# DeltaNet and soft-MoE on one Trainium2 core: another order for VectorE's queue, an own tile for half of the inverse, another start

## The chip, the cores and the metric

The kernel runs on one core of one Trainium2 chip. A time is device microseconds of one execution; a kernel's time is the median of its runs. A profiled run is one such execution with a trace, and its span is about 1.7 us shorter than its time. Runs count as slow when they are over 1.5% above the fastest of the same kernel; slow runs stay out of ratios, but medians take in all runs. PE is TensorE, DVE is VectorE, ACT is ScalarE, POOL is GpSimd, SP is SyncE; SPq is SyncE's DMA queue.

## The reference, cut to what matters

```python
# q, k, v: (B=4, H=8, S=768, D=48) float32, beta: (4, 8, 768)
k_n = k / (norm(k, axis=-1) + 1e-6)
for t in range(S):                          # one state of 48x48 per (b, h)
    y[:, :, t] = q[:, :, t] . state
    v_old = state . k_n[:, :, t]
    state = state + beta[t] * outer(k_n[t], v[t] - v_old)
x = y, transposed to (3072, 384)
# soft mixture of experts: 8 experts, 4 slots each, hidden size 1024
logits = x @ phi                            # (3072, 32)
d = softmax(logits, axis=0); slot_input = d.T @ x
slot_out[e] = relu(slot_input[e] @ w1[e]) @ w2[e]
out = softmax(logits, axis=1) @ slot_out
```

## The kernel before

The sequence is cut into 24 chunks of 32 tokens. Within a chunk the recurrence becomes a triangular system of 32x32, and its inverse is built on VectorE for four chunks (a group) at a time, one group ahead. A chunk itself is a chain over four engines:

```python
rest()      # PE: psR = K . S (state), then DVE: R = V - psR
read()      # PE: psY = Q . S
solve()     # PE: psR = inverse . R ; ACT: U = psR
update()    # PE: psS += K^T . U    ; ACT: S = psS   (the next chunk's state)
outputs()   # PE: psY += A . U      ; ACT: Y = psY
```

R is VectorE's only step in that chain. VectorE's other work is the inverse: 95 instructions for each group, products `prE`, `prM`, `prL` and the additions of them, then two back transposes; the preparation of the next inverse (a spreading transpose `lb`, the norms of k, which need a square root from ScalarE); and steps of the routing.

```python
# the second half of the inverse: a product, then its addition, 16 times
def la(j):
    tt = full(st["tt"])
    pr["l", j] = outer("prL", [HC - j, HC], tt[:, HC + j:C, HC + j].unsqueeze(2),
                       st["nm"][:, j, :].unsqueeze(1))      # outer: tile tag, bufs=2
def ls(j):
    add(full(st["tt"])[:, HC + j:C, 0:HC], pr["l", j], ALU.add)

# which share of the inverse's steps stands in which of a chunk's three places
share = [(0.0, 0.10, 0.11), (0.11, 0.10, 0.10), (0.09, 0.08, 0.08), (0.11, 0.12, 0.0)]

# one chunk of the main loop, in the order in which each engine's queue is filled
hook("head")                    # routing
drain(EL[c][0])                 # inverse, place 0; for c == 0 the norms come first
rest(); read()
...
hook("act"); drain(EL[c][1])    # routing, then inverse, place 1
if follow and x > GC:
    follow[0]["spread"]()
solve()
...
hook("mid"); hook("vec")
drain(EL[c][2])                 # inverse, place 2
update(); outputs()
...
# query blocks that chunk x asks for
queries = {0: (), 1: (9, 10, 11), 2: (12, 13), 3: (14,), 4: (15, 16)}
```

At the start the first loads go to SyncE and ScalarE, beta comes in 16 small loads on GpSimd, and V0 to V3 are loaded by SyncE. At the end the experts' weights `w1t` and `w2t` (15 loads of 1.5 MB) take memory that the loop's buffers leave.

Of the kernel before, what the change touches and what calls it, by code (L numbers as in the profile page):

```python
# [16 lines left out]
def kernel(  # L17
# [83 lines left out]
    load_k(2, nc.scalar)  # L101
    load_k(1)
    load_k(3, nc.scalar)

    one = cpool.tile([P, 1], F32, name="one")
    nc.vector.memset(one, 1.0)
    nc.scalar.preload_act_table_set("natural_log_exp_and_others")
    load_q(0)
    load_k(4)
    load_q(4)  # L110
    load_v(0)
# [18 lines left out]

    bb = cpool.tile([P, NG, C], F32, name="bb")
    for h in range(4):
        for c in range(GC):
            p0 = C * h + U * c
            nc.gpsimd.dma_start(
                out=bb[p0:p0 + U],
                in_=beta.rearrange("b (g h) (n c t) -> h c (b g) n t", h=4, c=GC, t=C)[h, c])
# [10 lines left out]

    psS = psp.tile([P, 4, 512], F32, name="psS")
    psR = psp.tile([P, 512], F32, name="psR")  # L150
    psY = psp.tile([P, 512], F32, name="psY")
    St = [wk.tile([P, 4, B, GD], F32, name=f"S{i}", bufs=1) for i in range(2)]
    for t in St:
        nc.vector.memset(t, 0.0)
# [76 lines left out]
    def invert(n):  # L231
# [17 lines left out]
        def clear():  # L249
            st["nm"] = wk.tile([P, HC, HC], F32, name="nm", tag="nm", bufs=1)  # L250
            nc.gpsimd.memset(st["nm"], 0.0)  # L251
# [54 lines left out]
        def steps():  # L306
# [27 lines left out]
            def la(j):  # L334
                tt = full(st["tt"])
                pr["l", j] = outer("prL", [HC - j, HC], tt[:, HC + j:C, HC + j].unsqueeze(2),
                                   st["nm"][:, j, :].unsqueeze(1))

            def ls(j):
                add(full(st["tt"])[:, HC + j:C, 0:HC], pr["l", j], ALU.add)  # L340
# [11 lines left out]
            for j in range(HC + 1):  # L352
                if j < HC:
                    put(HC * (HC - j), lambda j=j: la(j))
                if j > 0:
                    put(HC * (HC + 1 - j), lambda j=j - 1: ls(j))
            return out
# [117 lines left out]
    def route(n, Yn, yT):  # L475
# [103 lines left out]
        def collect(first):  # L579
# [4 lines left out]
            else:  # L584
# [5 lines left out]
                dict(head=[maxima], mid=[over_rows, by_tokens], vec=[rows_max, over_slots],  # L590
                     end=[spread_max, slots_exp]),
                dict(head=[run_max, shares], act=[rows_exp], end=[repeat, heads]),
# [17 lines left out]
    share = [(0.0, 0.10, 0.11), (0.11, 0.10, 0.10), (0.09, 0.08, 0.08), (0.11, 0.12, 0.0)]  # L610

    def plan(n):
# [3 lines left out]
        if n > 1:  # L616
            at[0][0] += [f["norms"]]
        todo, done, total = f["steps"], 0.0, 0.0
        whole = sum(t[0] for t in todo)
        i = 0  # L620
        for c in range(GC):
            for p in range(PLACES):
                total += share[c][p] * whole
                while i < len(todo) and done + todo[i][0] / 2 < total:
                    done += todo[i][0]
                    at[c][p].append(todo[i][1])
                    i += 1
        at[2][2] += [lambda: f["back"](0)]
        at[3][1] += [t[1] for t in todo[i:]]
        at[3][2] += [lambda: f["back"](1)]  # L630
# [5 lines left out]
    pre = {}  # L636
    f0 = invert(0)
    f0["unit"]()
    for cc in range(4):
        pre[cc] = Prep(cc)  # L640
        pre[cc].alone(0, cc % 2)
        if cc:
            pre[cc - 1].products(0, 1)
    pre[3].products(0, 1)
    f0["spread"]()
    f0["root"]()
# [3 lines left out]
    load_v(1)  # L650
# [16 lines left out]
    load_v(2)  # L667
    load_q(3)
    load_k(9)
    load_v(3)  # L670
# [32 lines left out]
    queries = {0: (), 1: (9, 10, 11), 2: (12, 13), 3: (14,), 4: (15, 16)}  # L703
# [8 lines left out]
    for x in range(NCH):  # L712
# [23 lines left out]
        rest, solve, read, update, outputs = chunk(x, Ys[n % 2])  # L736
        hook("head")
        drain(EL[c][0])
# [5 lines left out]
        if x == 0:  # L744
            f["spread"]()
            f["root"]()
            f["norms"]()
        hook("act")
        drain(EL[c][1])
        if follow and x > GC:  # L750
            follow[0]["spread"]()
# [8 lines left out]
        hook("mid")  # L760
        hook("vec")
        if follow and x < GC:
            follow[0]["spread"]()
        drain(EL[c][2])
# [166 lines left out]
```

## Time and profile before

| | before |
|---|---|
| time, median of 3 runs | 383.27 us (376.66 to 384.48) |
| span of the profiled run | 377.8 us, state fast |
| busy: PE, DVE, ACT, POOL | 77%, 59%, 44%, 41% |
| R of chunk 0 starts at | 47.14 us |
| four chunks each, from 0, 4, 8, 12, 16 | 53.33, 43.76, 42.56, 44.43, 37.62 us |
| chunks 20 to 23, no inverse beside them | 22.03 us for three |
| R of chunk 23 to the end (the tail) | 86.93 us |

The table cuts the span at the starts of R, because each chunk has one, 24 in the span. "R(8)" below is the start of R of chunk 8. One more line of the page is needed later. It is the row of moved GB/s in the 40 equal slices of the span (9.4 us each here); the experts' weights are the high figures from the 32nd slice on:

```profile
GB/s 104 92 83 91 81 85 86 89 90 62 80 51 57 50 70 97 88 109 106 35 19 25 23 27 23 13 13 190 3 4 14 391 427 341 340 424 399 6 201 299
```

### The profile page before, as it was taken

The numbers are of one execution on the slowest core, as the hardware profiler recorded it, in microseconds if no ns is written. First come the engines' busy times: TensorE is split into PE (matmuls) and PEld (weight loads), VectorE is DVE, ScalarE is ACT, GpSimd is POOL, SyncE is SP. The second block draws the span as 40 slices with busy tenths as digits, with TensorE's granted clock in tenths as the row PEclk, the third lists the DMA queues.
The fourth block names the chain that finished last, engine by engine and source line by source line (L and its number), as shares of the span: only waits on it lengthen the run. The fifth ranks groups of instructions, "written<-read, shape, count | busy, mean of one in ns | idle before, by whom it ended". The sixth has DMA issues, their size and how long they took to land.

```text
span 377.8 us, 16079 instructions
## 1 busy us (share of the span) xinstructions
PE 289.3 (77%) x6879; PEld 227.0 (60%) x6879; DVE 223.1 (59%) x798; ACT 164.4 (44%) x340; POOL 154.6 (41%) x338
## 2 busy tenths in 40 slices
PE   1866585789587997779787795789988779867784
PEld 0655474677476886668676794677877673312242
DVE  7289989087757777689847987879321120101043
ACT  1353154366356582668454572446466312001032
POOL 8453478564665059350975039856220000000000
PEclk9996569689799698999989898968999969979895
DMA  6555555553433344554111111005000998899058
GB/s 104 92 83 91 81 85 86 89 90 62 80 51 57 50 70 97 88 109 106 35 19 25 23 27 23 13 13 190 3 4 14 391 427 341 340 424 399 6 201 299
DMA packets 85030, 45.23 MB, mean 120 GB/s; under 512 B 79424, under 2 KB 82656, under 8 KB 83040
## 3 DMA queue, kind: packets, MB, share of 16 engines
q1 hardware_dynamic: 82208, 43.67, 43.1%
q8 instruction: 54, 0.88, 1.0%
q10 hardware_dynamic: 2176, 0.39, 0.7%
q0 software_dynamic: 576, 0.15, 0.3%
q14 instruction: 16, 0.13, 0.1%
HBM read 39.47 MB, written 4.72 MB: 117 GB/s over the span
## 4 chain that ended last, share of the span: by engine, by line
PE 48%; DMA 13%; ACT 12%; DVE 12%; SPq 9%; issue 4%; DVEq 0%; ACTq 0%
PE psR L423 8%; SPq L82 7%; PE psS L436 7%; DMA w2t<-in_moe_w_dram 6%; PE pt L574 5%; PE psY L453 4%; ACT S L443 4%; PE pt L194 4%; DMA Q<-in_q_dram 4%; PE pt L471 4%; PE pso L869 3%; PE pt L223 3%; PE psR L409 2%; DVE R L416 2%; PE ph L845 2%
## 5 line engine op out<-in xcount | busy, mean ns | idle before, releaser
L373 POOL TENSOR_SCALAR V<-V,nT 128x48 f32<-128x48 f32 x192 | 89.0, 487 | 38.5 <-DMA V<-in_v_dram 23.7
L381 POOL TENSOR_SCALAR_AFFINE_SELECT Ab<-GQ 32x256 f32<-32x256 f32 x96 | 46.0, 479 | 28.0 <-PE psY L453 23.7
L423 PE MATMUL psR<-R,Tb 64*64 64x48 f32 x768 | 32.1, 241 | 30.0 <-DVE R L416 18.7
L423 PEld LDWEIGHTS psR<-R,Tb 64*64 64x64 f32 x768 | 29.4, 156 | 33.7 <-issue 21.4
L443 ACT ACTIVATE S<-psS 48x768 f32<-48x768 f32 x46 | 37.0, 805 | 27.2 <-PE psS L436 26.9
L223 PE MATMUL pt<-KQ 48*32 48x64 f32 (+1 forms) x1792 | 26.3, 237 | 10.9 <-ACT KQ L210 7.8
L426 ACT ACTIVATE U<-psR 128x384 f32<-128x384 f32 x24 | 11.8, 491 | 51.2 <-PE psR L423 51.2
L223 PEld LDWEIGHTS pt<-KQ 48*32 48x32 f32 x1792 | 21.2, 119 | 17.1 <-ACT KQ L210 9.3
L299 DVE TENSOR_TENSOR prL<-tt,nm 128x256 f32<-128x256 f32 (+7 forms) x96 | 29.1, 308 | 3.1
L453 PE MATMUL psY<-U,Ab 64*64 64x48 f32 x768 | 30.0, 232 | 0.1
L304 DVE TENSOR_TENSOR nm<-nm,prM 128x16 f32<-128x16 f32 (+7 forms) x96 | 29.8, 310 | 0.0
L299 DVE TENSOR_TENSOR prM<-tt,lb 128x16 f32<-128x16 f32 (+7 forms) x96 | 29.4, 306 | 0.1
L304 DVE TENSOR_TENSOR tt<-tt,prL 128x256 f32<-128x256 f32 (+7 forms) x96 | 29.2, 304 | 0.2
L453 PEld LDWEIGHTS psY<-U,Ab 64*64 64x64 f32 x768 | 27.0, 147 | 2.8 <-issue 1.0
L436 PE MATMUL psS<-U,K 32*112 32x96 f32 x736 | 27.9, 296 | 0.1
L436 PEld LDWEIGHTS psS<-U,K 32*112 32x112 f32 x736 | 23.8, 200 | 4.8 <-issue 1.4
L416 DVE TENSOR_TENSOR R<-V,psR 128x384 f32<-128x384 f32 x24 | 13.0, 543 | 21.2 <-PE psR L409 10.3
L227 ACT ACTIVATE GQ<-pt 128x256 f32<-128x256 f32 (+1 forms) x56 | 16.7, 351 | 20.2 <-PE pt L223 20.1
L194 PE MATMUL pt<-ident,Q 128*128 128x128 f32 x72 | 20.4, 317 | 6.6 <-DMA Q<-in_q_dram 6.6
L386 ACT ACTIVATE Tb<-TT,own 128x256 f32<-128x256 f32 x48 | 21.6, 503 | 7.8 <-DVE TT L364 7.8
L299 DVE TENSOR_TENSOR prE<-tt,lb 128x30 f32<-128x30 f32 (+7 forms) x90 | 24.6, 273 | 0.0
L251 POOL MEMSET nm<- 128x256 f32 x6 | 1.9, 311 | 54.5 <-DVE tt L304 51.2
(132 smaller groups left out, 545.9 us busy)
## 6 DMA issues: line engine op xcount, KB each, us to landing
w2t<-in_moe_w_dram SPq DMA_DIRECT2D x8, 1536.0 KB, 19.4
w1t<-in_moe_w_dram SPq DMA_DIRECT2D x7, 1536.0 KB, 11.0
Q<-in_q_dram SPq DMA_DIRECT2D x96, 48.0 KB, 2.7
V<-in_v_dram SPq DMA_DIRECT2D x96, 48.0 KB, 2.4
out_dram<-ob SPq DMA_DIRECT2D x24, 192.0 KB, 2.4
K<-in_k_dram SPq DMA_DIRECT2D x88, 48.0 KB, 2.6
w1t<-in_moe_w_dram SPq DMA_DIRECT2D x3, 512.0 KB, 4.3
K<-in_k_dram ACTq DMA_DIRECT2D x8, 48.0 KB, 3.3
```

The source lines that it names most:

```text
L82: eng.dma_start(out=dst[C * h:C * h + C, :, 0:D], in_=src.rearrange("b (g h) s d -> h s (b g) d", h=4)[h, cc * C:(cc + 1) * C])
L194: nc.tensor.transpose(dst, self.src[a][:, b * G:(b + 1) * G, :].rearrange("p g d -> p (g d)"), ident)
L223: nc.tensor.matmul(pg[g][rh, b], lhsT=kq[r, b, 0, rh], rhs=kq[r, b, a0:a1, rh], start=True, stop=True, skip_group_check=True)
L299: nc.vector.tensor_tensor(pr, a.broadcast_to([P] + shape), b.broadcast_to([P] + shape), op=ALU.mult)
L304: nc.vector.tensor_tensor(dst, dst, pr, op=op)
L373: nc.gpsimd.tensor_scalar(Vt[cc][:, u], Vt[cc][:, u], nT[n][:, c * U + u:c * U + u + 1], None, op0=ALU.mult)
L381: nc.gpsimd.affine_select(out=Ab[cc % NT][r, :, h % 2, :].rearrange("p (b g) t -> p b g t", g=G), in_=GQ[n][r, c, :, :, 1, :], compare_op= ...
L386: nc.scalar.activation(Tb[cc % 2][:, :, x, :], TT[n][:, c * U:(c + 1) * U, :], ACT.Identity, scale=own[:, x:x + 1])
L423: nc.tensor.matmul(pw[half[y], u], lhsT=T[y][:, u], rhs=st["R"][half[y], u], start=(u == 0), stop=True, skip_group_check=True)
L436: nc.tensor.matmul(psS[0:DP + D, h, b * GD:(b + 1) * GD], lhsT=K[hs[h], b * G:(b + 1) * G].rearrange("p g d -> p (g d)")[:, 0:DP + D], rhs ...
L443: nc.scalar.activation(new[r, :, :, g * D:(g + 1) * D], psS[r, :, 0:B * GD].rearrange("p h (b g e) -> p h b g e", b=B, g=G)[:, :, :, g], A ...
L453: nc.tensor.matmul(qs[half[y], b, g], lhsT=at[y][:, u], rhs=st["U"][half[y], u], start=False, stop=True, skip_group_check=True)
```

## The change

The intent is to let nothing stand in VectorE's queue before R that could stand behind it. Before R there remain a share of the inverse's steps and the little routing that stays in "head"; norms, row maxima and slot shares come behind it. The spread moves to the end of the last place. The second half of the inverse gets a tile of its own, `T21`, so that its additions don't write `tt`. At the start, block K3 and V0 to V3 go to GpSimd's queue, beta comes in one load (`bt`), is laid out by PE with a selection matrix (`sel`), and two products of zeros are given to PE before its first block. Query block 9 is asked for a chunk earlier.

```diff
@@ start
 load_k(0)
 load_k(2, nc.scalar)
+load_k(3, nc.gpsimd)
 load_k(1)
-load_k(3, nc.scalar)
...
+bt = wk.tile([C, S], F32, name="bt", tag="dr", bufs=1)
+nc.sync.dma_start(out=bt, in_=beta.rearrange("b h s -> (b h) s"))
-load_v(0)
...
+sel = wk.tile([C, GC, 4, GC, U], F32, name="sel", tag="dT", bufs=1)
...                                    # sel is filled from ident
-for h in range(4):
-    for c in range(GC):
-        nc.gpsimd.dma_start(out=bb[p0:p0 + U], in_=...)      # 16 small loads
+load_v(0, nc.gpsimd)                   # V1, V2, V3 follow the same way
+def blocks_of_beta():                  # called between spread and root
+    pb = pt([P, NG, C])
+    for c in range(GC):
+        nc.tensor.matmul(pb, lhsT=sel[:, c]..., rhs=bt...[:, c], ...)
+    nc.scalar.activation(bb, pb, ACT.Copy)
+for i in range(2):                     # St[0] is zero here
+    nc.tensor.matmul(psS[:, i], lhsT=z[:, 0:P], rhs=z[:, 0:512], start=True, stop=True)
@@ inverse
-    pr["l", j] = outer("prL", ...)     # all j
+    if j == 0: T21 = the product itself
+    else:      pr["l", j] = outer("prL", [HC - j, HC], a, b)
-    add(full(st["tt"])[:, HC + j:C, 0:HC], pr["l", j], ALU.add)
+    add(st["T21"][:, j:HC, :], pr["l", j], ALU.add)          # from j = 1
+    put(HC * HC, join)                 # one copy of T21 into tt
@@ order
-share = [(0.0, 0.10, 0.11), (0.11, 0.10, 0.10), (0.09, 0.08, 0.08), (0.11, 0.12, 0.0)]
+share = [(0.0, 0.08, 0.13), (0.10, 0.09, 0.11), (0.10, 0.06, 0.09), (0.10, 0.14, 0.0)]
-    at[0][0] += [f["norms"]]           # before R of chunk c = 0
+    at[0][1] += [norms]                # behind it
-queries = {0: (), 1: (9, 10, 11), ...
+queries = {0: (9,), 1: (10, 11), ...
-hook("head")
 drain(EL[c][0])
+hook("head")
-if follow and x > GC:
-    follow[0]["spread"]()
...
+drain(EL[c][2][:cut])
 hook("vec")
-drain(EL[c][2])
+drain(EL[c][2][cut:])
+if follow:
+    follow[0]["spread"]()
```

In the routing, the row maxima and the slot shares move from "head" to "act", behind R. Not shown above: the second back transpose of the inverse moves up by one place.

More of the change, by code (lines that the diff above doesn't have):

```diff
@@ L101 @@
     load_k(2, nc.scalar)
+    load_k(3, nc.gpsimd)
     load_k(1)
-    load_k(3, nc.scalar)
     one = cpool.tile([P, 1], F32, name="one")
     nc.vector.memset(one, 1.0)
+    St = [wk.tile([P, 4, B, GD], F32, name=f"S{i}", bufs=1) for i in range(2)]
+    nc.vector.memset(St[0], 0.0)
     nc.scalar.preload_act_table_set("natural_log_exp_and_others")
+    bt = wk.tile([C, S], F32, name="bt", tag="dr", bufs=1)
+    nc.sync.dma_start(out=bt, in_=beta.rearrange("b h s -> (b h) s"))
     load_q(0)
@@ L128 @@
     nc.vector.tensor_reduce(own, hm.rearrange("p (y x) -> p x y", x=2), axis=AX.X, op=ALU.add)
-    bb = cpool.tile([P, NG, C], F32, name="bb")
-    for h in range(4):
-        for c in range(GC):
-            p0 = C * h + U * c
-            nc.gpsimd.dma_start(
-                out=bb[p0:p0 + U],
-                in_=beta.rearrange("b (g h) (n c t) -> h c (b g) n t", h=4, c=GC, t=C)[h, c])
+    sel = wk.tile([C, GC, 4, GC, U], F32, name="sel", tag="dT", bufs=1)
+    nc.vector.memset(sel, 0.0)
+    for c in range(GC):
+        nc.vector.tensor_copy(sel[:, c, :, c, :],
+                              ident[0:C, 0:C].rearrange("k (u h) -> k h u", h=4))
+    bb = cpool.tile([P, NG, C], F32, name="bb")
+    load_v(0, nc.gpsimd)
     phi = cpool.tile([GD, 4, NSL], F32, name="phi")
@@ L147 @@
     load_k(7)
+    def blocks_of_beta():
+        pb = pt([P, NG, C])
+        for c in range(GC):
+            nc.tensor.matmul(pb, lhsT=sel[:, c].rearrange("k h c u -> k (h c u)"),
+                             rhs=bt.rearrange("k (n c t) -> k c n t", c=GC, t=C)[:, c],
+                             start=(c == 0), stop=(c == GC - 1))
+        nc.scalar.activation(bb, pb, ACT.Copy)
+    load_v(1, nc.gpsimd)
     psS = psp.tile([P, 4, 512], F32, name="psS")
@@ L151 @@
     psY = psp.tile([P, 512], F32, name="psY")
-    St = [wk.tile([P, 4, B, GD], F32, name=f"S{i}", bufs=1) for i in range(2)]
-    for t in St:
-        nc.vector.memset(t, 0.0)
+    nc.vector.memset(St[1], 0.0)
     NT = 3
@@ L250, in clear @@
             st["nm"] = wk.tile([P, HC, HC], F32, name="nm", tag="nm", bufs=1)
+            st["T21"] = wk.tile([P, HC, HC], F32, name="T21", tag="T21", bufs=1)
             nc.gpsimd.memset(st["nm"], 0.0)
@@ L334, in la, with join @@
             def la(j):
-                tt = full(st["tt"])
-                pr["l", j] = outer("prL", [HC - j, HC], tt[:, HC + j:C, HC + j].unsqueeze(2),
-                                   st["nm"][:, j, :].unsqueeze(1))
+                a, b = full(st["tt"])[:, HC + j:C, HC + j].unsqueeze(2), st["nm"][:, j, :].unsqueeze(1)
+                if j == 0:
+                    nc.vector.tensor_tensor(st["T21"], a.broadcast_to([P, HC, HC]),
+                                            b.broadcast_to([P, HC, HC]), op=ALU.mult)
+                else:
+                    pr["l", j] = outer("prL", [HC - j, HC], a, b)
             def ls(j):
-                add(full(st["tt"])[:, HC + j:C, 0:HC], pr["l", j], ALU.add)
+                add(st["T21"][:, j:HC, :], pr["l", j], ALU.add)
+            def join():
+                nc.vector.tensor_copy(full(st["tt"])[:, HC:C, 0:HC], st["T21"])
             for j in range(HC):
@@ L354, in steps @@
                     put(HC * (HC - j), lambda j=j: la(j))
-                if j > 0:
+                if j > 1:
                     put(HC * (HC + 1 - j), lambda j=j - 1: ls(j))
+            put(HC * HC, join)
             return out
@@ L589, in route @@
         return [dict(end=[logits]),
-                dict(head=[maxima], mid=[over_rows, by_tokens], vec=[rows_max, over_slots],
+                dict(act=[maxima], mid=[over_rows, by_tokens], vec=[rows_max, over_slots],
                      end=[spread_max, slots_exp]),
-                dict(head=[run_max, shares], act=[rows_exp], end=[repeat, heads]),
+                dict(head=[run_max], act=[rows_exp, shares], end=[repeat, heads]),
                 dict(end=[lambda: slots((0, 1))]),
@@ L615, in plan @@
         at = [[[] for _ in range(PLACES)] for _ in range(GC)]
-        if n > 1:
-            at[0][0] += [f["norms"]]
         todo, done, total = f["steps"], 0.0, 0.0
         whole = sum(t[0] for t in todo)
+        norms = f["norms"]
         i = 0
@@ L627, in plan @@
                     i += 1
+                if not (c or p):
+                    at[0][1] += [norms]
         at[2][2] += [lambda: f["back"](0)]
-        at[3][1] += [t[1] for t in todo[i:]]
-        at[3][2] += [lambda: f["back"](1)]
+        at[3][1] += [t[1] for t in todo[i:]] + [lambda: f["back"](1)]
         return f, at
@@ L636 @@
     pre = {}
+    for i in range(2):
+        z = St[0].rearrange("p h b e -> p (h b e)")
+        nc.tensor.matmul(psS[:, i], lhsT=z[:, 0:P], rhs=z[:, 0:512], start=True, stop=True)
     f0 = invert(0)
     f0["unit"]()
+    load_v(2, nc.gpsimd)
+    load_v(3, nc.gpsimd)
     for cc in range(4):
@@ L645 @@
     f0["spread"]()
+    blocks_of_beta()
     f0["root"]()
@@ L649 @@
     load_q(7)
-    load_v(1)
     f0["clear"]()
@@ L666 @@
     load_q(8)
-    load_v(2)
     load_q(3)
     load_k(9)
-    load_v(3)
     load_k(10)
@@ L702 @@
              2: ("", "t10 u10", "p10 t11"), 3: ("u11", "p11 t12", "u12")}
-    queries = {0: (), 1: (9, 10, 11), 2: (12, 13), 3: (14,), 4: (15, 16)}
+    queries = {0: (9,), 1: (10, 11), 2: (12, 13), 3: (14,), 4: (15, 16)}
     def later(x, place):
@@ L736 @@
         rest, solve, read, update, outputs = chunk(x, Ys[n % 2])
+        drain(EL[c][0])
         hook("head")
-        drain(EL[c][0])
         rest()
@@ L746 @@
             f["root"]()
-            f["norms"]()
         hook("act")
         drain(EL[c][1])
-        if follow and x > GC:
-            follow[0]["spread"]()
         solve()
@@ L760 @@
         hook("mid")
+        cut = (len(EL[c][2]) + 1) // 2
+        drain(EL[c][2][:cut])
         hook("vec")
-        if follow and x < GC:
+        drain(EL[c][2][cut:])
+        if follow:
             follow[0]["spread"]()
-        drain(EL[c][2])
         update()
```

## The prediction

> **What bounds the kernel now.** I read the page's busy shares first (PE 77%, DVE 59%: no engine is full over the whole span of 377.8 us), so the span had to be cut into stages. The starts of the R subtraction (the VectorE step between reading the state and solving a chunk, x24) mark the 24 chunks. R starts at 47.1, 100.5, 144.2, 186.8, 231.2 and 268.8 us for chunks 0, 4, 8, 12, 16 and 20. The view of busy time by stretch, cut there (columns: length, busy us of PE, weight loads, DVE, ACT, POOL, granted clock, DMA share, GB/s):
>
> ```profile
> 47.14:100.47 53.33, 38.86 (x1144) 33.45 (x1144) 37.38 (x126) 27.69 (x59) 35.12 (x74) 0.82 0.51 83
> 144.23:186.79 42.56, 35.56 (x1058) 31.01 (x1058) 33.74 (x126) 25.30 (x52) 22.31 (x53) 0.96 0.46 91
> 268.84:305.00 36.16, 29.61 (x788) 25.61 (x778) 7.54 (x27) 19.02 (x37) 2.30 (x7) 0.98 0.35 141
> ```
>
> Four chunks with the 95-instruction inverse beside them take 42.6 us; chunks 20 to 23, which have no inverse, follow each other in 7.0 to 7.8 us, that is 30 per four. So the loop is held by VectorE's in-order queue: R stands behind other VectorE work. The timeline of chunks 7 to 8 shows it:
>
> ```profile
> 140.06 0.87 PE L409 MATMUL psR<-S,KQ 128*32 128x96 f32 x32
> 141.04 0.35 DVE L274 RECIPROCAL rn<-nrm 128x32 f32<-128x32 f32 x1 [0.61 <-ACT nrm L267]
> 143.10 1.08 DVE L283 TENSOR_TENSOR lb<-lb,gm 128x512 f32<-128x512 f32 x2
> 144.11 0.20 DVE L287 STREAM_TRANSPOSE nT<-nrm 128x32 f32<-128x32 f32 x1
> 144.23 0.51 DVE L416 TENSOR_TENSOR R<-V,psR 128x384 f32<-128x384 f32 x1
> 144.88 1.14 PE L423 MATMUL psR<-R,Tb 64*64 64x48 f32 x32 [2.51 <-DVE prE L299]
> ```
>
> The state's product is there at 140.9, but the norms of the next inverse (141.04 to 144.23) run before R, and PE idles 2.5 us. VectorE also idles within a group, on routing steps placed too early (its waits, chunks 8 to 11):
>
> ```profile
> DVE sacc L581 <- PE pt L574: 2.3, 1, 2.3
> DVE m L491 <- ACT lT L487: 1.7, 1, 1.7
> DVE mr L504 <- PE pt L496: 1.2, 1, 1.2
> DVE sacc L585 <- PE pt L574: 1.0, 1, 1.0
> ```
>
> All its waits there sum to 7.8 us. Chunks 0 to 3 have another fault, in the chain of waits:
>
> ```profile
> 63.83 0.90 SPq L82
> ...
> 66.25 2.44 DMA Q<-in_q_dram
> 68.83 1.73 PE pt L194 x7
> 70.56 1.75 PE psS L436 x32
> 72.31 1.88 PE psY L453 x32
> ```
>
> PE waits 4.9 us for query block 9, issued at 64.8 because SyncE's queue works with hardly a pause from 0.8 to 61.6 us (four issues of about 0.47 us a block). After it PE runs cold: the state update takes 1.75 us where the warm one takes 0.97.
>
> Before chunk 0 the chain is VectorE: the first spread at 16.98, norms to 22.9, inverse 0 without a gap to 47.3. The spread waits for four K blocks, of which the second starts PE only at 9.39. The tail hangs on chunk 23: SyncE's waits show
>
> ```profile
> SPq L172 <- DVE R L416: 33.3, 1, 33.3
> ```
>
> so the expert weights (15 loads of 1.5 MB, 23.6 MB) start when R of chunk 23 has read V (291.4 us), run at 341 to 427 GB/s to 351.6, and are followed by 26 us of last products and stores. The tail therefore moves with R of chunk 23, one for one.
>
> [...] four 128x128 transposes take 1.09 us up to 22.8 us, 0.64 us from 23.7 us on, and are slow again after the 4.9 us stall. [...] Here issue time is what SyncE lacks (0.47 us each, 61 us on end), while the DMA engines are only 51 to 61% busy to chunk 4, so moving issues should help. [...] (a 128x240 add into strided tt 0.40 us, a 128x240 product into contiguous prL 0.40), so a contiguous tile gains nothing by its layout.
>
> **The change part by part.** The built program's order of instructions gives each engine's queue; the durations are start-to-start steps of VectorE in chunks 8 to 11 with waits taken out.
>
> *Second half in its own tile.* First add dropped (0.45 us), one copy added (about 0.35): nothing. It might have freed the products from waiting for the add before them, but in the built program each still waits for that same add, since its double-buffered product tile was last read there. Zero.
>
> *Order by slot.* VectorE work between R's, before: 8.36, 8.20, 7.82, 10.35 us for c = 0..3, plus idle 4.0, 2.43, 0, 1.4: 12.36 + 10.63 + 7.82 + 11.75 = 42.56. After:
> - c=0: R 0.45, norms 3.07 (moved here from before R), 37 inverse steps 7.32, sacc 0.18: 11.0. Its waits vanish: slots are ready at about R+6, the VectorE queue reaches sacc at R+7.4; the row maximum m moves behind the next R, where lT has long been there.
> - c=1: R 0.47, m 0.2, 24 steps 5.61, slot maxima 0.8, running maximum 0.35: 7.4, with some 0.5 left of waits 7.9; PE has the next state product at R+7.6 (164.2 against 156.6). 8.2.
> - c=2: R 0.46, shares 1.2, the rest of the inverse 5.98, first back transpose 0.93: 8.6, R follows at 8.7 (PE: 7.0).
> - c=3: R 0.47, 16 steps 3.31, join 0.35, transpose 0.93, spread and ssq 2.1, sacc 0.31: 7.5; PE's state product comes at R+8.5 (183.55 against 175.04). 8.9 instead of 11.75.
>
> Sum 36.8, with 0.5 for strays 37.3. Chunks 8 to 11 gain 5.3. Chunks 4 to 7 (43.76, with a 4.0 us wait for lT) gain 6.2, 12 to 15 (44.43, more cold PE) 6.5. Chunks 16 to 19 take up their own norms but have no spread: 11.0 + 8.2 + 8.7 + 7.0 = 34.9 against 37.6, gain 2.5.
>
> *Chunks 0 to 3.* Query block 9 now stands before V and K 13, and blocks V0 to V3 leave SyncE's queue: by the issue times 3.24 + 2.99 + 1.92 + 2.65 earlier, another 5.7 for the order, 0.5 later for beta: issued near 49 instead of 64.8, needed near 61. The stall goes, and the cold stretch behind it. By the same sums: 13.9 (was 14.1), 7.8 (was 15.7), 8.6 (9.6), 9.4 (14.0, norms gone): 39.7 against 53.3, gain 13.6.
>
> *Start.* K1 comes perhaps 0.7 us earlier (the eight first SyncE issues share the time with eight of ACT at 0.7 us each; now four). Two 512-column products of zeros before the first block may have PE warm: the K blocks then follow at about 1.3 instead of 1.87 us. 0.7 to 2.7, say 1.8. GpSimd's K3 issues push ident to about 4.6 us, still before 6.06. Beta's four products and one ACT copy lie beside the 1.9 us spread.
>
> Sum: 1.8 + 13.6 + 6.2 + 5.3 + 6.5 + 2.5 = 35.9 us. Chunks 20 to 23 and the tail: unchanged.
>
> **The rivals.**
> 1. PE takes over. It was busy 35.6 of 42.6 us, part of it cold; a warm pass over four chunks and their routing is 33 us by my sum of durations, and 37.3 leaves little for its own waits (U, S, psum slots). For it: c=3 is already PE's in my table. Against: 7.0 to 7.8 us a chunk without the inverse. If every chunk lost 0.5 us: 10 us given back, some 357.
> 2. The norms and routing are only moved: VectorE's 34 us a group remain, and any new wait in its queue costs as before. If half of the idle stays, 8 to 12 us come back: 355 to 359.
> 3. The early V blocks on GpSimd's queue crowd the DMA engines or delay ident, so the first K blocks land later: start +1 to 3 us instead of -1.8; then 350 to 352. Against: the first four K blocks are issued before them.
> 4. The tail is not tied to R of chunk 23 (PE's chain to 329 us frees the last weight buffers): the gain still reaches it, as that chain also starts at chunk 23.
>
> **Range and chances.** 383.3 - 35.9 = 347.4. Such sums rarely come whole; I keep about 92% of the gain: 350. Low end: all of it and a start warm throughout, from the faster before-runs (376.7 - 36): 341. High end: rivals 1 and 2 together in part: 361. The before-runs themselves differ by 2%. Faster by over 2% means below 375.6, which needs only the stall and one third of the loop: 0.96; same 0.03; slower 0.01.
>
> **What would show it.** Right: no PE wait for Q near chunk 1, and R(0) to R(4) near 40 us; no norms right before R of chunks 4, 8, 12, 16; R to R of chunks 8 to 12 near 37; VectorE's waits per group at 2 to 3 us instead of 7.8; the inverse's steps at the same durations; about 109 us from R(20) to the end, as before. Wrong: groups of 40 us or more with R waiting for PE, a first spread later than 17 us, new waits of R on V or POOL, or products of the second half that no longer wait for the add.

## The result

| | before | after |
|---|---|---|
| time, median of 4 runs each | 380.84 us (376.66 to 384.48) | 356.14 us (354.12 to 359.47) |
| span of the profiled run | 377.8 us, fast | 357.7 us, slow |
| R(0) | 47.14 | 48.32 |
| chunks 0-3, 4-7, 8-11, 12-15, 16-19 | 53.33, 43.76, 42.56, 44.43, 37.62 | 41.60, 36.34, 39.84, 35.60, 40.43 |
| R(20) to R(23) | 22.03 | 21.46 |
| tail | 86.93 | 94.11 |

The ratio is 0.9415 (95% interval 0.9278 to 0.9553): faster. Ratios here are the mean time of one kernel's fast runs over that of the other's of the same rounds, so not quite the ratio of the medians. The median lies inside the predicted range, 6 us above the predicted 350. The profiled run of the changed kernel happened to be its slowest, so a second profile of the same kernel was taken (the first experiment). The start and the tail below are alike in both; single chunks are not, as that experiment says.

The stages of the changed kernel, in the view of busy time by stretch (columns as in the prediction; chunks 8 to 11, 12 to 15, 16 to 19):

```profile
126.26:166.10 39.84, 35.88 (x1070) 31.34 (x1062) 34.30 (x125) 25.29 (x53) 27.40 (x61) 0.96 0.51 103
166.10:201.70 35.60, 33.02 (x1074) 28.96 (x1062) 34.03 (x125) 23.69 (x49) 18.89 (x43) 1.00 0.15 26
201.70:242.13 40.43, 32.91 (x758) 29.43 (x762) 32.90 (x125) 18.63 (x36) 31.14 (x63) 0.79 0.21 56
```

VectorE's busy time per group is what it was, 34 us, and chunks 12 to 15 need hardly more than that. Chunks 16 to 19 have fewer PE products, yet take longer, at a granted clock of 0.79.

The order came out as planned: in VectorE's timeline at chunk 16 the norms follow R.

```profile
201.70 0.54 DVE L436 TENSOR_TENSOR R<-V,psR 128x384 f32<-128x384 f32 x1
202.17 0.34 DVE L287 RECIPROCAL rn<-nrm 128x32 f32<-128x32 f32 x1
```

VectorE's waits in chunks 8 to 11, 7.8 us before, are 4.0 us (total, times, longest):

```profile
DVE sacc L605 <- PE pt L594: 2.9, 1, 2.9
DVE R L436 <- PE psR L429: 0.4, 1, 0.4
DVE R L436 <- POOL Ab L401: 0.4, 1, 0.4
DVE R L436 <- DMA K<-in_k_dram: 0.3, 1, 0.3
```

The waits for row maxima and exponentials are gone. One wait stays, for the slots' products, which my working had put at nothing.

PE's wait for query block 9 is gone, and the state update of chunk 1, cold before (1.75 us in the chain of waits, 1.82 in the timeline), runs warm:

```profile
66.99 1.04 PE L456 MATMUL psS<-U,K 32*112 32x96 f32 x32
```

"Cold" and "warm" name only the longer and the shorter of the times that the same PE products take in these traces: 1.82 and 1.04 us for the 32 of a state update, 1.95 and 1.14 for the 32 of a solve, 1.09 and 0.64 for four 128x128 transposes. Some take a time between the two.

**The start** became 1.2 us longer instead of 1.8 shorter. The first spread begins at 17.51 instead of 16.98, and from there to the first step of the inverse it takes 6.58 us (24.09 - 17.51) where it took 5.90 (22.88 - 16.98). Inverse 0 itself, with its transposes, is unchanged, 24.23 us against 24.26. The timeline of the changed kernel's start, all engines:

```profile
16.18 0.83 PE L235 MATMUL pt<-KQ 48*32 48x32 f32 x57 [0.79 <-issue]
17.36 2.92 PE L157 MATMUL pt<-bt,sel 32*128 32x192 f32 x8 [0.35 <-ACT GQ L239]
20.32 0.33 ACT L160 ACTIVATE bb<-pt 128x192 f32<-128x192 f32 x1 [2.84 <-PE pt L157]
20.55 0.22 ACT L279 ACTIVATE nrm<-ssq 128x32 f32<-128x32 f32 x1
21.06 0.35 DVE L287 RECIPROCAL rn<-nrm 128x32 f32<-128x32 f32 x1 [1.43 <-ACT nrm L280]
```

and the same two last steps before:

```profile
19.14 0.23 ACT L266 ACTIVATE nrm<-ssq 128x32 f32<-128x32 f32 x1 [2.19 <-DVE ssq L262]
19.66 0.35 DVE L274 RECIPROCAL rn<-nrm 128x32 f32<-128x32 f32 x1 [0.56 <-ACT nrm L267]
```

The prediction had laid beta's four products beside the 1.9 us spread. They take 2.92 us on a cold PE (the four transposes right behind them take 1.11 us), and the copy of their result stands in ScalarE's queue ahead of the logarithm that the norms wait for: the copy starts at 20.32, the logarithm at 20.55, though its input was there from 19.64 on (19.45 + 0.19).

**The tail** became 7.2 us longer. SyncE's timeline, where the weights of the first experts are issued, before:

```profile
293.24 2.04 SPq L178 DMA_DIRECT2D w2t<-in_moe_w_dram  x4
```

and after, with the longest waits of that queue:

```profile
264.28 0.82 SPq L184 DMA_DIRECT2D w1t<-in_moe_w_dram  x2
282.81 2.03 SPq L190 DMA_DIRECT2D w2t<-in_moe_w_dram  x4
...
SPq L190 <- PE pt L594: 17.6, 1, 17.6
```

R(23) is at 290.9 us before and 263.6 after. Two loads still follow it at once (264.28), but the first `w2t` load now comes 19.2 us after R(23), where it came 2.4 after it. It waits 17.6 us for PE's last slots products, and the loads behind it in the queue come after it (four `w2t` issues from 282.81 to 284.84, the next `w1t` at 284.88). The GB/s row of the page shows the hole at the 30th to 32nd slices (8.9 us each):

```profile
GB/s 132 160 95 82 87 93 58 50 81 73 84 74 81 71 123 121 105 116 28 5 31 31 38 4 23 190 14 5 4 119 237 86 431 426 423 426 322 2 220 307
```

The transfers run at 423 to 431 GB/s behind it, without the dip to 340 of before, which gives part of the delay back: 16.8 us later in issue became 7.2 us in the end.

The reason can be read in the built programs' memory layout. `bt` and `sel` carry the tags `dr` and `dT`, the buffers of the routing's last steps, so as to cost no memory. They are allocated first of all, so `dr` and `dT` now lie at bytes 91,360 to 97,504 of each partition, inside the first `w2t` buffer (85,728 to 98,016). Before, they were allocated late and lay at 215,648 to 221,792, where no weight comes early; the place inside `w2t` held `Tb` and `Ab`, free soon after R(23). Now the first `w2t` load has to wait until the last slots product has read `dr`.

### The profile page after: what moved, and what is told of

The parts are those of the page before. It is cut to its first block, busy times and chain, and to the rows that moved or that the text cites. A ratio compares the mean times of both kernels' runs of the same rounds, so it can differ in the third digit from the quotient of the medians.

```text
span 357.7 us, 16101 instructions
## 1 busy us (share of the span) xinstructions
PE 284.5 (80%) x6891; PEld 221.2 (62%) x6891; DVE 225.9 (63%) x803; ACT 163.3 (46%) x341; POOL 159.4 (45%) x342
## 4 chain that ended last, share of the span: by engine, by line
PE 41%; DVE 31%; DMA 13%; ACT 8%; issue 4%; SPq 2%; DVEq 0%; ACTq 0%
DMA w2t<-in_moe_w_dram 12%; PE psR L443 6%; PE psS L456 5%; PE psY L473 4%; PE pso L892 4%; PE pt L594 3%; DVE prE L312 3%; PE pt L235 3%; PE psR L429 3%; DVE nm L317 3%; PE pt L206 3%; DVE prM L312 3%; DVE prL L312 3%; DVE tt L317 3%; PE pt L491 3%
## 5 line engine op out<-in xcount | busy, mean ns | idle before, releaser
L401 POOL TENSOR_SCALAR_AFFINE_SELECT Ab<-GQ 32x256 f32<-32x256 f32 x96 | 47.6, 496 | 21.0 <-PE psY L473 16.7
L443 PE MATMUL psR<-R,Tb 64*64 64x48 f32 x768 | 30.0, 228 | 15.6 <-DVE R L436 11.6
L443 PEld LDWEIGHTS psR<-R,Tb 64*64 64x64 f32 x768 | 26.8, 142 | 19.3 <-issue 12.6
L473 PE MATMUL psY<-U,Ab 64*64 64x48 f32 x768 | 29.0, 228 | 0.1
L312 DVE TENSOR_TENSOR prL<-tt,nm 128x240 f32<-128x240 f32 (+14 forms) x90 | 26.3, 298 | 2.7
L473 PEld LDWEIGHTS psY<-U,Ab 64*64 64x64 f32 x768 | 25.9, 142 | 2.8 <-issue 0.7
L317 DVE TENSOR_TENSOR T<-T,prL 128x240 f32<-128x240 f32 (+14 forms) x90 | 26.2, 291 | 0.2
L317 DVE TENSOR_TENSOR tt<-tt,prE 128x30 f32<-128x30 f32 (+7 forms) x90 | 25.9, 288 | 0.0
L312 DVE TENSOR_TENSOR prE<-tt,lb 128x30 f32<-128x30 f32 (+7 forms) x90 | 25.4, 282 | 0.0
```

The lines of the kernel that those rows point to most:

```text
L312: nc.vector.tensor_tensor(pr, a.broadcast_to([P] + shape), b.broadcast_to([P] + shape), op=ALU.mult)
L317: nc.vector.tensor_tensor(dst, dst, pr, op=op)
L401: nc.gpsimd.affine_select(out=Ab[cc % NT][r, :, h % 2, :].rearrange("p (b g) t -> p b g t", g=G), in_=GQ[n][r, c, :, :, 1, :], compare_op= ...
L443: nc.tensor.matmul(pw[half[y], u], lhsT=T[y][:, u], rhs=st["R"][half[y], u], start=(u == 0), stop=True, skip_group_check=True)
L473: nc.tensor.matmul(qs[half[y], b, g], lhsT=at[y][:, u], rhs=st["U"][half[y], u], start=False, stop=True, skip_group_check=True)
```

## The experiments

Twelve runs were made, all with correct results; the first is the changed kernel itself. The table has, from the profiled run of each, the stages as above; variants' line numbers differ by a few from those of the changed kernel.

| run | time, median of 6 | ratio to before | R(0) | 0-3 | 4-7 | 8-11 | 12-15 | 16-19 | tail | profile's state |
|---|---|---|---|---|---|---|---|---|---|---|
| e0_after | 356.13 | 0.940 | 48.22 | 40.31 | 40.67 | 38.42 | 36.26 | 40.41 | 94.34 | slow |
| e1_tags | 348.36 | 0.923 | 48.85 | 40.15 | 37.84 | 37.91 | 36.12 | 36.70 | 86.46 | fast |
| e2_prl3 | 355.15 | 0.939 | 46.92 | 41.53 | 39.65 | 40.78 | 35.14 | 36.65 | 93.46 | slow |
| e3_no_own_tile | 356.61 | 0.945 | 48.53 | 40.38 | 40.93 | 37.61 | 35.45 | 37.11 | 93.12 | fast |
| e4_order_only | 356.17 | 0.930 | 46.89 | 47.05 | 39.50 | 36.58 | 36.65 | 36.95 | 89.16 | slow |
| e5_q9_only | 373.77 | 0.987 | 46.68 | 45.28 | 41.67 | 43.29 | 45.39 | 38.44 | 88.82 | fast |
| e6_tags_late | 351.56 | none | 48.02 | 41.26 | 37.77 | 38.94 | 35.40 | 37.07 | 88.87 | slow |
| e9_prl3_no_own | 353.86 | 0.934 | 47.21 | 40.03 | 40.55 | 37.53 | 35.17 | 37.28 | 93.26 | fast |
| e11_old_beta | 354.05 | 0.941 | 49.71 | 41.72 | 41.22 | 36.91 | 35.95 | 37.67 | 88.41 | fast |
| e12_best | 345.28 | 0.916 | 46.79 | 39.99 | 35.54 | 37.37 | 35.40 | 40.29 | 87.25 | fast |
| e13_old_beta_prl3 | 349.24 | 0.927 | 48.15 | 41.26 | 39.12 | 37.24 | 35.34 | 38.63 | 86.94 | fast |
| e14_best_nowarm | 346.56 | 0.920 | 46.58 | 39.97 | 39.22 | 37.49 | 35.38 | 40.33 | 87.57 | slow |

Runs e0 to e3 shared one chip and the runs of before there (median 379.62), e4, e5, e6 and e9 another job (381.44), e11 to e14 a third (380.71). The record's verdict is faster for e0, e1 and e2; e6 has none, and the others are called unclear, although only e5's interval reaches 0.98. The record gives no reason. e4's ratio rests on two fast runs.

**e0_after: the changed kernel again, no edit.**

> The changed kernel once more, as the yardstick for the other three on the same chip. Expected near 355 us (354.1 to 359.5 in the first four runs). If the 7 us that the stage after chunk 20 took longer are a matter of this program and not of one slow run, R of chunk 23 to the end is again near 94 us here (86.9 in the kernel before), with the first w2 load issued only when the last slot product is done. If they belonged to the one slow run, it is 87 to 89 us.

Measured: 356.13 us, ratio 0.940 (0.932 to 0.948), tail 94.34 and R(0) 48.22. Both losses, start and tail, are there again. The groups scatter, though: chunks 4 to 7 took 40.67 us here and 36.34 in the other profile, and nearly all of it is one chunk, chunk 5, 12.22 us against 7.83. PE's timeline at its solve, in the first profile and then in this one:

```profile
101.94 1.14 PE L443 MATMUL psR<-R,Tb 64*64 64x48 f32 x32 [2.62 <-DVE R L436]
```

```profile
100.56 1.94 PE L443 MATMUL psR<-R,Tb 64*64 64x48 f32 x32 [2.89 <-DVE R L436]
```

PE waits 2.6 to 2.9 us for R, and then its 32 products of the solve take 1.14 us in the one and 1.94 in the other, in the same program. In this profile VectorE's routing steps then wait 1.06, 0.63 and 1.81 us for PE's products; in the first they don't wait there. In these two profiles some 4 us go with it. It is not all: in e4 PE runs warm at that solve (1.14 us), and chunk 5 still takes 11.15.

**e1_tags: `bt` and `sel` in buffers of their own.**

```diff
-bt = wk.tile([C, S], F32, name="bt", tag="dr", bufs=1)
+bt = wk.tile([C, S], F32, name="bt", bufs=1)
-sel = wk.tile([C, GC, 4, GC, U], F32, name="sel", tag="dT", bufs=1)
+sel = wk.tile([C, GC, 4, GC, U], F32, name="sel", bufs=1)
```

> The tiles of beta (bt, sel) get buffers of their own instead of the names dr and dT; nothing else. Theory: because bt and sel are allocated first, the shared buffers of dr and dT moved from the end of the pool into the bytes of the first w2 load, which therefore waits for the last reader of dr (the last slot product) and holds up every load queued behind it. Then here: no such wait, w2 loads issued within 2 us of the w1 loads, R of chunk 23 to the end back to 87 us, time 5 to 8 us below e0 (about 348). Rival A (the new tile T21 shifted the layout): no change here, and e3 restores the tail. Rival B (a cold or slow run): no change here, and e0 already has a short tail.

Measured: 348.36 us, ratio 0.923 (0.916 to 0.931); 7.8 us below e0 by the medians of the same job, 6.3 by the means of the fast runs. The tail is 86.46, that of before. In SyncE's timeline the `w2t` load follows the `w1t` loads at once, and the GB/s row has no hole:

```profile
259.73 1.01 SPq L184 DMA_DIRECT2D w1t<-in_moe_w_dram  x2
260.79 2.01 SPq L190 DMA_DIRECT2D w2t<-in_moe_w_dram  x4
```

```profile
GB/s 130 153 104 81 68 99 66 74 78 85 76 78 51 68 78 136 131 132 62 28 25 29 28 26 24 18 193 5 5 4 313 428 424 230 426 428 304 2 241 305
```

The edit changes nothing but the place of two tiles. It costs 5 KB a partition, which were free. So the shared tags were the tail's loss, as far as it stands out of the scatter (86.9 to 89.2 us in before, e4 and e5, which don't have these tiles).

**e2_prl3: three buffers for `prL` instead of two.**

```diff
-pr = wk.tile([P, HC * HC], F32, name=tag, tag=tag, bufs=2)
+pr = wk.tile([P, HC * HC], F32, name=tag, tag=tag, bufs=3 if tag == "prL" else 2)
```

> Three buffers instead of two for the products prL of the second half of the inverse; nothing else. Theory of the prediction: the own tile freed nothing because each product still waits for the add just before it, the last reader of its buffer. Then with a third buffer a product overlaps the add: about 13 hand-overs of 0.13 us in each of 6 inverses, 1.7 us less VectorE time per inverse (10 us in all), of which the first inverse (1.7 us, before chunk 0, all on the path) and a part of the five others reach the end: 4 to 8 us below e0. Rival: the wait is only nominal [...], then the steps keep their 0.13 us gaps and the time is that of e0 within 1 us.

Measured: 355.15 us, ratio 0.939 (0.932 to 0.945), 1 us below e0 and inside its scatter. The step that I expected did get shorter. In the built program no product waits on the addition before it (78 did in the changed kernel), and the second half of inverse 0, from the first `prL` to the back transposes, takes 6.57 us (38.58 to 45.15) instead of 8.11 (38.45 to 46.56). R(0) is 1.3 us earlier. In the loop, chunks 14 and 15 take 7.64 and 7.36 us against 8.30 and 7.67. These two are the chunks of a group in which the second half stands, so a group has 1.0 us to gain, and the scatter of the other chunks hides it. My expectation for the total missed.

**e3_no_own_tile: without `T21`,** the additions go into `tt` as before and the copy falls away; all else as changed.

```diff
-add(st["T21"][:, j:HC, :], pr["l", j], ALU.add)
+add(full(st["tt"])[:, HC + j:C, 0:HC], pr["l", j], ALU.add)
-put(HC * HC, join)
```

> The second half is added into the inverse's tile again, as in the kernel before; everything else as changed. Theory of the prediction: the own tile is worth nothing (one add less, one copy more, same waits): within 1 us of e0, and R to R in chunks 4 to 12 as in e0. Rival (the own tile lets product and add overlap or makes the adds cheaper): 3 to 10 us slower than e0. For the tail: if the layout moved because of T21, the tail shortens to 87 us here; by the theory of e1 it stays at 94.

Measured: 356.61 us, ratio 0.945 (0.936 to 0.954), against 0.940 (0.932 to 0.948) of e0: no difference clear of noise. The own tile is worth nothing that these runs show, and the tail of 93.12 shows that its memory was not what moved the weights.

**e9_prl3_no_own: both edits together.**

> Three prL buffers and no own tile (the second half added into tt as in the kernel before). In the built program the product's wait for the add goes here too, so the buffer count, not the tile, carries the wait. Expected: the same time as e2 within 1 us, 4 to 8 us below the changed kernel. Rival (both are needed): time of the changed kernel.

Measured: 353.86 us, ratio 0.934 (0.929 to 0.940), R(0) 47.21. That is 2.3 us below e0 by the medians (of another job), not the 4 to 8 expected. The wait falls away without the own tile too: 6 are left of 78. VectorE's timeline in the second half of inverse 0, changed kernel, then this one:

```profile
40.49 0.37 DVE L317 TENSOR_TENSOR T<-T,prL 128x208 f32<-128x208 f32 x1
40.89 0.34 DVE L312 TENSOR_TENSOR prL<-tt,nm 128x176 f32<-128x176 f32 x1
```

```profile
40.41 0.39 DVE L316 TENSOR_TENSOR tt<-tt,prL 128x224 f32<-128x224 f32 x1
40.72 0.35 DVE L311 TENSOR_TENSOR prL<-tt,nm 128x192 f32<-128x192 f32 x1
```

The held product starts 0.03 us after the addition's end (40.49 + 0.37 = 40.86); the one that waits for nothing starts 0.08 us before it. That is the whole worth of the third buffer: 0.1 us, some 15 times an inverse.

**e4_order_only: the kernel before with the order alone:** the order hunk of the diff, without `queries`, the own tile and the start (the norms of group 1 stay where they were).

> The kernel before with only VectorE's order by slot (steps, R, norms, routing, spread, second back transpose, shares of the steps); loads, beta, inverse tile as before. By the prediction's sums the order is worth 4.8 (norms before R of chunk 4) + 6.2 + 5.3 + 6.5 + 2.5 = 25 us; the trace of the changed kernel gave less in chunks 8 to 19, so 18 to 25 us expected: 356 to 363, with the stall for query block 9 still there and the tail at 87 us. Rival (the gain came from the loads, the order only moved work): under 8 us.

Measured: 356.17 us, ratio 0.930 (0.919 to 0.942), as much as the whole change. From R(0) to R(20) it takes 196.7 us, 25.0 less than before (221.7). By stages the five parts, from chunks 0 to 3 on, are 6.3, 4.3, 6.0, 7.8 and 0.7 us. R(0) is near that of before, the tail 2.2 us longer. PE's wait for query block 9 is there, as it should be:

```profile
69.01 0.45 PE L194 MATMUL pt<-ident,Q 128*128 128x128 f32 x1 [5.98 <-DMA Q<-in_q_dram]
```

**e5_q9_only: the kernel before with the query block alone.**

```diff
-queries = {0: (), 1: (9, 10, 11), 2: (12, 13), 3: (14,), 4: (15, 16)}
+queries = {0: (9,), 1: (10, 11), 2: (12, 13), 3: (14,), 4: (15, 16)}
```

> The kernel before with one edit: query block 9 is issued in chunk 0, ahead of V4 and K13, instead of in chunk 1. Its issue moves from 64.8 to about 59 us, so it lands near 62 against the 63.7 at which PE wants it: the 4.9 us wait goes, and part of the cold stretch after it; 4 to 8 us faster than before in R(0) to R(4). Rival: later loads (10, 11) then stall PE in chunk 2 instead, or VectorE holds R(2) anyway: under 2 us.

Measured: 373.77 us, ratio 0.987 (0.980 to 0.995): 7.7 us less by the medians, but these take in slow runs of both, most of all of before; by the means of the fast runs it is 4.8. R(1) to R(2) takes 8.80 us instead of 15.68, and chunks 0 to 3 lose 8.05. The other groups scatter by up to 2.1 us against the profile of before, so the 8.05 are not exact. By the fast runs, one line moved by one chunk is worth nearly a fifth of what the whole new order is (4.8 against 26.3 us).

**e6_tags_late: as e1, and beta's products recorded after the root.**

```diff
 f0["spread"]()
-blocks_of_beta()
 f0["root"]()
+blocks_of_beta()
 f0["norms"]()
```

> e1 and in addition the beta products recorded after the two ScalarE steps of the first norms, so that ScalarE's copy of bb no longer stands ahead of them. In the changed kernel the first Ln waited until 20.55 us for that copy, 0.9 us after ssq was ready; gm needs bb only 1.5 us after the first reciprocal. Expected: the first inverse starts 0.5 to 0.9 us earlier than in e1, the time 0.3 to 1 us below e1. Rival: the copy of bb then holds gm instead, and nothing is gained.

Measured: median 351.56 us; one run was 344.68 and the five others over 1.5% above it, so they count as slow and no ratio is given. The timeline settles the question of the start instead: from the spread to the first step of the inverse it takes 5.80 us (17.86 to 23.66), where the six profiles with beta ahead of the root (after, e0, e1, e2, e3, e9) take 6.58 or 6.59. The place of the copy is thus worth 0.8 us. The other part, the late spread, is untouched.

**e11_old_beta: the changed kernel with beta's 16 small loads back,** without `bt`, `sel` and their products.

> The changed kernel with only the beta part undone: sixteen small GpSimd loads write bb as before, no bt, no sel, no beta products on PE. In the built program dr and dT lie last again, and the first w2t load waits on the same semaphores as in the kernel before. Theory (the new beta path costs the tail through the shared tiles, and the start through the bb copy that stands ahead of the Ln on ScalarE): R(23) to the end back to 87 to 89 us (94.1 in the changed kernel), R(0) at 47.1 to 47.6 instead of 48.3, loop as in the changed kernel, total 346 to 350. Rival (the tail's growth comes from something else in the change, such as the V blocks on GpSimd's queue): tail stays at 93 to 94 and total 355 to 357. Rival for the start (the PE stop inside the K3 products sets it, whatever beta does): R(0) stays at 48 or more.

Measured: 354.05 us, ratio 0.941 (0.935 to 0.948). The tail is back at 88.41 with the V blocks still on GpSimd's queue, so these have no part in its growth. R(0), however, is 49.71, later instead of earlier, and here the expectation fell, that for the total too (346 to 350). The spread begins early, at 16.00, and the inverse with it, at 22.70. Then its fourth step stops (VectorE's timeline, then GpSimd's):

```profile
25.72 0.19 DVE L307 TENSOR_TENSOR nm<-nm,prM 128x16 f32<-128x16 f32 x1 [2.58 <-POOL nm L254]
```

```profile
25.36 0.33 POOL L254 MEMSET nm<- 128x256 f32 x1
```

GpSimd clears `nm` at 25.36 because its queue has to issue 16 loads of beta at 0.55 to 0.58 us each and then the V blocks that the change gave it; in the changed kernel it does so at 16.51. So beta's one load was needed for the V blocks to go to GpSimd: the two parts of the start belong together.

**e12_best: everything that helped:** the buffers of e1, beta late as in e6, three `prL` buffers, no own tile.

> Both repairs together with three prL buffers and without the own tile: bt and sel in buffers of their own, beta's products recorded after the root, prL with three buffers. If the gains add (7.8 us of the tail from the run with own buffers, 1 to 2 us of the first inverse from the third buffer): 344 to 348, R(0) 46.5 to 47.2, tail 86.5. If the third buffer gives nothing once the tail is repaired, because the loop is then held by PE: 348 to 350.

Measured: 345.28 us, ratio 0.916 (0.909 to 0.923). R(0) is 46.79, the tail 87.25. This is the fastest kernel of the study, though its interval overlaps those of e1 and e14.

One kernel was not run: the new order and the query block alone, with the start and the inverse of before. If the gains of e4 and e5 add, its ratio would be 1 - 0.070 - 0.013 = 0.917; this is an estimate from those two runs. It equals what e12 has (0.916) with the new start, both repairs and the third buffer. And R(0) was 46.7 to 47.1 us with the start of before (before, e4, e5), 48.0 with the new one mended (e6); e12's 46.79 also holds the third buffer's 1.3. So no run shows that the new start gained anything.

**e14_best_nowarm: e12 without the two zero products.**

```diff
-for i in range(2):
-    z = St[0].rearrange("p h b e -> p (h b e)")
-    nc.tensor.matmul(psS[:, i], lhsT=z[:, 0:P], rhs=z[:, 0:512], start=True, stop=True)
```

> The run before it in this job (own buffers for bt and sel, beta after the root, three prL buffers, no own tile) without the two zero products. If the warm-up is worth the 1.3 us that my prediction gave it: total and R(0) later by 1 to 1.5 us than that run. If it is worth nothing, since [...] the start is held by the K3 block: same R(0) within 0.3 us. The PE stop inside the K3 products, which stands at a fixed instruction in all variants with warm-up, should move by the two instructions taken away if it is a matter of instruction count, and go if it comes from the zero products.

Measured: 346.56 us, ratio 0.920 (0.912 to 0.928). The intervals of e12 and e14 overlap, and R(0) is 46.58 against 46.79: the warm-up is worth nothing measurable. The stop that PE makes inside the products of block K3 is there without it too; this is PE's timeline of e14:

```profile
14.53 0.43 PE L235 MATMUL pt<-KQ 48*32 48x32 f32 x11 [0.36 <-ACT GQ L239]
16.69 0.80 PE L235 MATMUL pt<-KQ 48*32 48x32 f32 x53 [1.72 <-issue]
```

In the changed kernel and in e12 the stop comes after 7 of the 64 products, here after 11. Four is the number of records that the two zero products have in the changed kernel's profile. In all ten profiles that have it, 219 records of PE's products stand before it. So where it comes, it stands at a fixed count of PE's instructions, and the profile shows no wait for data. What makes it is not settled: in e13, with the zero products, it isn't there (the 64 products run in 1.32 us). The kernel before shows no stop there (its 64 products run in 1.10 us).

**e13_old_beta_prl3: e11 with three `prL` buffers and no own tile.**

> The beta part undone as in the first run of this job, and in addition three prL buffers and no own tile. If the sixteen small loads are the better path at the start: R(0) 45.5 to 46.3, tail 87 to 89, total 343 to 347, at or below the run with both repairs. If they are the worse one: GpSimd's sixteen issues delay its own memsets, the V blocks and phi, R(0) no earlier, total 347 to 351.

Measured: 349.24 us, ratio 0.927 (0.921 to 0.934), R(0) 48.15, tail 86.94. The first inverse's wait for GpSimd is 2.2 us here. It is 4.0 us above e12 by the medians, 1.4 of them at R(0); with the V blocks on GpSimd's queue, beta's one load is the better start, once its tiles lie elsewhere. Against the start of before, with V0 to V3 on SyncE's queue, it was not tested.

## Why the prediction was right or wrong

The chance of 0.96 for faster was right, and the range held the median. That it did is in part luck: its high end was set for rivals 1 and 2, and much of the loss came from the start and the tail. The sum of parts was less right. Set against the one profile of each kernel (spans 377.8 and 357.7, 20.1 us apart), the 35.9 us come out like this:

| part | predicted | measured in the profile | off by |
|---|---|---|---|
| start | -1.8 | +1.2 | 3.0 |
| chunks 0-3 | -13.6 | -11.7 | 1.9 |
| chunks 4-7 | -6.2 | -7.4 (e0: -3.1) | -1.2 |
| chunks 8-11 | -5.3 | -2.7 (e0: -4.1) | 2.6 |
| chunks 12-15 | -6.5 | -8.8 | -2.3 |
| chunks 16-19 | -2.5 | +2.8 | 5.3 |
| chunks 20-22 | 0 | -0.6 | -0.6 |
| tail | 0 | +7.2 | 7.2 |
| sum | -35.9 | -20.0 | 15.9 |

Of the prediction's own signs of being wrong, some came: the first spread stood later than 17 us (17.51), in chunks 8 to 11 R waited 0.4 us for POOL, which it did not there before, and one group took over 40 (40.43), though not with R waiting for PE. Of its signs of being right, "about 109 us from R(20) to the end" failed (115.6). Two of its figures are a little off: 37.6 - 34.9 is 2.7, not 2.5, and chunks without the inverse follow each other in 6.7 to 7.7 us from R to R, not 7.0 to 7.8.

**The bound and the order.** Right in the mechanism. e4 isolates the order, and its loop is 25.0 us shorter. My sum for it was 6.2 + 5.3 + 6.5 + 2.5 = 20.5 us plus chunk 3's norms, 14.0 to 9.4 = 4.6: 25.1. That the two agree so closely is luck: by stages the sum is off by 0.7 to 1.9 us, in both directions (4.6, 6.2, 5.3, 6.5, 2.5 against 6.3, 4.3, 6.0, 7.8, 0.7). By single chunks, the table of c = 0 to 3 said 11.0, 8.2, 8.7 and 8.9; chunks 8 to 11 took 11.12, 8.47, 8.83 and 11.42, chunks 12 to 15 took 11.30, 8.33, 8.30 and 7.67. The first three are within 0.4 us in both groups; the fourth came out at 11.42 in the one, with a stop of PE of 1.10 us and cold products behind it (the state update took 1.82 us), and better than foretold in the other. The waits fell to 4.0 us, not to 2 to 3, because one for `sacc` stayed at 2.9.

**The query block.** Right: the stall is gone, worth 8.05 us in its four chunks alone (e5). In the kernel before, SyncE's four issues of a block took about 1.9 us, the transfer of query block 9 behind the last of them 2.44. Its place in that queue was enough to end the stall; what moving V0 to V3 to GpSimd's queue added, no run shows.

**The own tile.** Right in reason, and in amount within the noise (e3). e2 and e9 show that the number of `prL` buffers carried the wait.

**Chunks 16 to 19.** Wrong by 5.3 us in the profile, and in e0 and e12 as well. The terms 8.2 for chunk 17 and 7.0 for chunk 19 assumed a warm PE. In chunk 16 VectorE's 11.3 us, with no preparation left for PE to do, leave PE idle:

```profile
213.69 1.95 PE L443 MATMUL psR<-R,Tb 64*64 64x48 f32 x32 [3.75 <-DVE R L436]
```

and behind it chunk 17 took 10.37 us, much of it cold (the solve 1.95 us, the state update 1.83). Every profile of the new order has this wait (3.7 to 4.4 us), a state update of 1.82 or 1.83 us behind it, and 9.1 to 10.4 us for chunk 17, so even the best group took 36.65. The larger part is chunk 19, in the views by stretch of the changed kernel and of e1:

```profile
232.23:242.13 9.90, 9.20 (x184) 8.47 (x188) 5.25 (x21) 3.97 (x7) 3.83 (x9) 0.66 0.05 19
230.68:237.57 6.89, 6.18 (x184) 5.69 (x188) 5.26 (x20) 3.98 (x7) 4.28 (x10) 1.00 0.15 60
```

The same products took 3 us more at a granted clock of 0.66. The wait in chunk 16 doesn't decide this: in e9 PE was cold behind it (the solve took 1.94 us) and chunk 19 took 6.88 us, in e13 the solve was warm (1.14) and chunk 19 took 9.89. Nor does the wait's length: after 3.75 us alike the solve took 1.95 us in the changed kernel and 1.14 in e1. All twelve profiles of the new order agree in another thing: where PE was still cold at the solve of chunk 18 (1.41 to 1.84 us: e1, e2, e3, e4, e6, e9), chunk 19 took 6.9 us; where it was warm again (1.13 to 1.14 us: the changed kernel, e0, e11 to e14), 8.3 to 9.9. Why is not shown. e4 has the order alone, and its group took 36.95 us against 37.62 before; the prediction's 34.9 had no cold PE in it.

**Start.** The failed steps are two. "Beta's four products and one ACT copy lie beside the 1.9 us spread": they lie 2.92 us beside it on cold PE, and the copy holds the logarithm; 0.68 us, taken back in e6 and e12 (5.80 and 5.78 us from spread to inverse). "Two 512-column products of zeros before the first block may have PE warm": K1's block indeed came 0.5 us earlier (8.91 against 9.39), but PE ran its transposes at 1.09 to 1.12 us as before. That they would warm PE was a guess of mine. In e0, e3, e9, e11 and e13 some of them were warm (0.63 to 0.66 us), and so was one block in e14 without the two products. Their effect is thus not settled, but e14 shows no gain. With PE's stop of 0.79 us in K3's products the spread begins 0.53 us later. 0.53 + 0.68 = 1.21 us, all that R(0) lost.

**Tail.** "The tail therefore moves with R of chunk 23, one for one" is the step that failed. SyncE's wait that I quoted names what released the load that came first, R(23). It doesn't say that the loads behind it will find their memory free in the changed kernel. The sharing of buffers by tags was in the diff, and the layout could have been read in the built program before the run. e1 shows the loss: a tail of 86.46 us, where the changed kernel, e0, e2, e3 and e9 have 93.1 to 94.3.

The 92% that I kept stood for "PE takes over" and "norms only moved". The missing microseconds were mostly neither: 10.2 of the 15.9 lie in the start and the tail. The third rival had a longer start, but by another cause (e11 shows K1's transposes at 8.69 us with the V blocks on GpSimd, so the first blocks were not held up); rival 4 doubted that the tail is tied to R of chunk 23, but held that the gain reaches it all the same, and named another buffer's release. With both mended and the third buffer added, e12 is 31.6 us below the before of its job by the means of the fast runs (35.4 by the medians, where most runs of before are slow).

## What to carry to other kernels

In the kernel before, VectorE took R in its place in the queue, 3.3 us after the state's product was there (144.23 against 140.9, the norms between them). In such a queue, put the step that others wait for first and let everything else follow; here that alone was worth 25 us. A sum of instruction durations from the trace foretold the total, with errors of up to 1.9 us in its stages that cancelled. When a change gives a new tile an old tag, look where that tag's buffer now lies and what later takes that memory: a buffer allocated at the start held up a load near the end for 17.6 us, and a test with own buffers costs one line. Before a part is put "beside" other work, look at what stands behind it in its own engine's queue: the place of one copy was worth 0.8 us here (e6).
